# Stores on ScalarE's DMA queue, 25 words later: a fused agent attention and maxout FFN on one core

## The chip, the core and the metric

The kernel runs on one core of one Trainium2 chip. The core has a tensor engine (PE; PEld is its weight load), VectorE (DVE), ScalarE (ACT), GpSimd (POOL) and SyncE (SP), each with its own instruction stream that runs in program order. They meet through semaphores. Data moves between the chip's memory (HBM) and the on-chip SBUF through 16 DMA engines; a DMA is issued as an instruction in one engine's stream, and each issuing engine has a DMA queue of its own. Matmul results land in PSUM.

The metric is the device time of one execution, in microseconds (us): the median of several runs. The profile is of one further execution, and its span runs from the program's first instruction to its last.

## What is computed

```python
def _attn_ref(q, k, v, agents):                      # q, k, v: 4 x 12544 x 128, agents: 4 x 49 x 128
    def sm(a, b):                                    # softmax of scale * a b^T over the last axis
        ...
    agent_v = sm(agents, k) @ v                      # 49 x 128 for each batch
    return sm(q, agents) @ agent_v

def _moe_ref(x, w1, w2, w3, w_out):                  # x: 50176 x 128, w1..w3: 128 x 768, w_out: 768 x 128
    h = np.maximum(np.maximum(x @ w1, x @ w2), x @ w3)
    return h @ w_out
```

The attention's output, 50176 rows of 128, is the input of the FFN. q, k, v are read once and the output is written once, in fp32: four tensors of 25.7 MB each.

## The kernel before

Keys and values of the four batches (b = 0 to 3) are handled in tiles of 7 x 128 rows (`k*b.g`, `v*b.g`), up to four tiles to a load of 1792 KB. Out of them come, for each batch, the 49 agent values and a small matrix G that carries the whole FFN for queries of that batch. Queries are handled in groups s = 0 to 48 of 8 x 128 rows (group 48 holds the last two row blocks of all four batches). One load `ql.z` brings three groups (1536 KB); one store `st` takes three groups away.

A query group goes through these steps, each a word in the program's order:

- `qc` (GpSimd, line 535) casts the loaded rows to bf16; `qt` (PE, line 305) transposes; `qe` (ScalarE, line 541) evacuates.
- `sc` (PE, line 273) gives scores, `ex` (ScalarE, line 554) exponentials, `su` and `re` their sums and reciprocals (VectorE, line 564).
- `u` and `v` (PE) give the hidden values, `a` (ScalarE, line 574) and `x` (VectorE, line 577) the maximum, `p` (PE) the output products.
- `ov.s.0` and `ov.s.1` (VectorE, line 595; for `ov.47.1` ScalarE, line 598) scale them into the output tile OS.
- `st` (line 521, function `store`) issues the DMA from OS to the output. Groups 0 to 44 leave in fifteen stores of three groups (st.2, st.5, ... st.44), groups 45, 46 and 48 in stores of 512 KB, group 47 in two halves.

Loads go to five LD buffers and outputs to five OS buffers: the first `ov` of a new set of three groups waits until the store that last read its buffer has landed. All loads and stores are issued by SyncE, apart from one small load of the agents on ScalarE's queue (line 214).

The order is written out by hand as one text of 1225 words, `ORDER`. Every word is emitted in that order, so the place of a word fixes where its instruction stands in the stream of its engine, and only there: a word's neighbours on other engines do not hold it, semaphores do. A suffix such as `/4` names the buffer. The list `graph` tells each word's engine, its inputs and its tiles; the numbers `cost` and `serve` in it are not used when the order is given.

Of the kernel before, what the change touches and what calls it, by code (L numbers as in the profile page):

```python
# [197 lines left out]
class Emit:  # L198
# [316 lines left out]
    def store(self, s, h=None):  # L515
        def fn():
            n = LONG if s < NQ - 1 - TG else GT
            far, near = self.far("out", s, n), self.near(s, self.t[f"os.{s // TG * TG}"], n)
# [2 lines left out]
            self.nc.sync.dma_start(far, near)
        return fn
# [226 lines left out]
kx1.7/1 kv1.6 a.1/1 su.2 v.1/6 re.2 u.2/0 qc.3/0 kv1.7 x.1/1 a.2/2 v.2/4 p.1/3,1 qc.4/1 x.2/2 qt.3/2 ov.1.0 p.2/7,6 qc.5/2
qe.3/0 ov.1.1 kl1.12/4 ov.2.0 kc1.8/1 sc.3/0 ov.2.1 qt.4/4 ex.3/3 kc1.9/2 kt1.8/3 qe.4/1 vl1.12/1 su.3 u.3/1 ke1.8/1 v.3/2  # L750
kc1.10/0 kt1.9/7 a.3/0 re.3 ks1.8/6 sc.4/4 ke1.9/2 kx1.8/2 kc1.11/1 kt1.10/3 x.3/0 st.2 ex.4/4 ks1.9/0 qt.5/1 ke1.10/0 kx1.9/3
vc1.8/2 su.4 kt1.11/6 qe.5/2 re.4 ks1.10/7 p.3/2,0 ke1.11/1 vc1.9/3 kx1.10/0 kv1.8 ov.3.0/1 sc.5/3 vc1.10/0 kv1.9 ov.3.1
ex.5/5 ks1.11/4 ql.9/0 u.4/1 vc1.11/1 kx1.11/1 kv1.10 a.4/1 su.5 v.4/6 re.5 u.5/7 qc.6/0 kv1.11 x.4/1 a.5/2 v.5/2 p.4/0,4
x.5/2 qc.7/1 qt.6/3 ov.4.0 p.5/1,6 kc1.12/2 qe.6/0 kl2.0/2 ov.4.1 ov.5.0 kc1.13/0 kt1.12/7 sc.6/2 ov.5.1 qt.7/0 vc1.12/2
ke1.12/2 ex.6/6 kt1.13/4 qe.7/1 su.6 vc1.13/3 ks1.12/3 ke1.13/0 u.6/1 v.6/6 re.6 kx1.12/2 sc.7/7 qc.8/2 a.6/0 vl2.0/4 kv1.12
ex.7/7 ks1.13/0 x.6/0 kx1.13/3 qt.8/4 kv1.13 qe.8/2 su.7 p.6/2,3 nr1 u.7/1 v.7/6 re.7 ov.6.0/2 a.7/1 sc.8/0 pu1/4 ov.6.1 pv1/5
ex.8/0 ql.12/1 x.7/1 vs1 qc.9/0 su.8 u.8/7 ub1 v.8/1 re.8 a.8/2 p.7/2,3 tm1 qc.10/1 qt.9/5 ov.7.0 qe.9/0 qc.11/2 ov.7.1 x.8/2
sc.9/6 vb1 kl2.4/3 qt.10/0 rd1 ex.9/1 p.8/7,4 kc2.0/1 qe.10/1 su.9 u.9/2 v.9/3 kc2.1/2 kt2.0/5 a.9/0 sc.10/1 re.9 ke2.0/1
qt.11/0 kc2.2/0 ex.10/2 ov.8.0 kt2.1/2 qe.11/2 ks2.0/6 kc2.3/1 ov.8.1 su.10 kt2.2/5 vl2.4/0 ps1/7 re.10 kx2.0/0 ke2.1/2 u.10/4
pd1 sc.11/0 a.10/1 ke2.2/0 vc2.0/0 ks2.1/1 kt2.3/6 ex.11/3 sl1 ks2.2/2 kx2.1/1 v.10/4 vc2.1/1 kv2.0/5 kx2.2/2 ke2.3/1 su.11  # L760
px1/1 re.11 vc2.2/2 x.9/0 kv2.1 gx1 x.10/1 ks2.3/7 ql.15/2 py1/2 vc2.3/3 kx2.3/3 kv2.2 qc.12/0 gy1 kv2.3 p.9/6,0 qc.13/1
p.10/3,1 ov.9.0/3 qt.12/4 ov.9.1 u.11/7 qc.14/2 qe.12/0 v.11/2 kl2.8/4 ov.10.0 kc2.4/2 ov.10.1 a.11/2 sc.12/6 qt.13/0 x.11/2
ex.12/4 kc2.5/0 kt2.4/3 qe.13/1 su.12 p.11/4,7 ke2.4/2 kc2.6/1 kt2.5/1 re.12 ov.11.0 ks2.4/2 sc.13/0 kc2.7/2 kx2.4/0 ke2.5/0
vl2.8/1 kt2.6/3 ex.13/5 ov.11.1 qt.14/6 vc2.4/0 ks2.5/4 ke2.6/1 su.13 qe.14/2 kt2.7/2 u.12/1 re.13 vc2.5/1 ke2.7/2 kv2.4
kx2.5/1 ks2.6/7 sc.14/3 a.12/0 vc2.6/2 kv2.5 kx2.6/2 ks2.7/0 ex.14/6 v.12/6 vc2.7/3 u.13/2 kx2.7/3 x.12/0 kv2.6 ql.18/3 a.13/1
su.14 v.13/4 re.14 u.14/1 qc.15/0 x.13/1 kv2.7 a.14/2 p.12/7,0 qc.16/1 p.13/6,2 ov.12.0/4 qt.15/3 ov.12.1 qc.17/2 v.14/4
qe.15/0 ov.13.0 kl2.12/0 ov.13.1 sc.15/1 kc2.8/0 x.14/2 qt.16/7 ex.15/7 kc2.9/1 kt2.8/0 qe.16/1 vl2.12/2 su.15 p.14/6,3 ke2.8/0
# [71 lines left out]
```

## Time and profile before

| what | us |
|---|---|
| median of 3 runs | 259.56 (258.92 to 260.03) |
| profiled execution | 258.95 |
| its span | 257.1 |
| PE busy | 187.8 |
| VectorE busy | 166.3 |
| GpSimd busy | 145.6 |
| ScalarE busy | 145.2 |

In the profile an engine with a q behind its name (SPq, ACTq) is its sequencer, which waits and issues. A line of a timeline reads: start, duration, engine, line of the kernel, operation, tile written <- tiles read, shapes, count, and in brackets the idle time before it with what ended that. A line of a group or of the DMA issues ends with the time from issue to landing, which is when the last of the 16 DMA engines has finished its part. In the table of windows the last three columns are the tensor engine's granted clock, the mean busy share of the 16 DMA engines and the bytes that they moved per time.

### The profile page before, as it was taken

How to read it: one execution, taken by the hardware profiler on the slowest of the kernel's cores; microseconds unless marked ns; L12 is line 12 of the kernel's file. 1: busy time of each engine (PE TensorE's matmuls, PEld its weight loads, DVE VectorE, ACT ScalarE, POOL GpSimd, SP SyncE). 2: the span in 40 equal slices, each digit the busy share in tenths (PEclk: the TensorE clock that was granted, in tenths of full speed). 3: DMA queues.
4: the chain of work that ended last, by engine and by line, in shares of the span. 5: the costliest groups of instructions: out<-in, count | busy, mean ns of one | idle time of the engine just before them, and what ended most of it. 6: DMA issues, size and time to landing. Idle time of an engine off the chain costs nothing.

```text
span 257.1 us, 7504 instructions
## 1 busy us (share of the span) xinstructions
PE 187.8 (73%) x3071; PEld 138.0 (54%) x3106; DVE 166.3 (65%) x344; ACT 145.2 (56%) x240; POOL 145.6 (57%) x164
## 2 busy tenths in 40 slices
...
DMA  7999999999999999999999999999999999999992
GB/s 257 435 415 416 427 420 426 420 426 419 420 418 425 423 422 427 424 418 423 418 426 424 419 425 425 426 416 421 424 432 421 421 410 431 423 423 426 410 370 85
DMA packets 11528, 105.01 MB, mean 409 GB/s; under 512 B 1176, under 2 KB 2396, under 8 KB 4444
## 3 DMA queue, kind: packets, MB, share of 16 engines
q1 hardware_dynamic: 11280, 104.34, 97.0%
...
q10 hardware_dynamic: 203, 0.10, 0.1%
q14 instruction: 19, 0.15, 0.1%
...
## 4 chain that ended last, share of the span: by engine, by line
DMA 55%; POOL 12%; PE 12%; DVE 8%; ACT 5%; issue 3%; another core or an unknown queue 1%; SPq 0%; DVEq 0%; ACTq 0%; POOLq 0%
DMA LD<-in_v_dram 25%; DMA LD<-in_k_dram 14%; DMA out_dram<-OS 9%; PE psum L273 9%; POOL VB L300 6%; DMA LD<-in_moe_w_dram 5%; DVE OS L595 3%; POOL KB L300 3%; POOL QB L535 3%; PE psum L305 3%; DMA sums_of<-in_agents_dram 2%; ACT EQ L554 1%; ACT VB L298 1%; ACT QT L541 1%; DVE R L577 1%
## 5 line engine op out<-in xcount | busy, mean ns | idle before, releaser
L300 POOL CAST KB<-LD 128x896 bf16<-128x896 f32 x56 | 51.8, 964 | 36.2 <-DMA LD<-in_k_dram 35.2
L535 POOL CAST QB<-LD 128x1024 bf16<-128x1024 f32 x49 | 49.7, 1048 | 34.7 <-DMA LD<-in_q_dram 26.0
L595 DVE TENSOR_TENSOR OS<-psum,sums_of 128x512 f32<-128x512 f32 x97 | 60.7, 676 | 9.7 <-DMA out_dram<-OS 5.0
L541 ACT ACTIVATE QT<-psum 128x1024 bf16<-128x1024 bf16 x49 | 50.2, 1024 | 21.9 <-PE psum L305 20.2
L311 DVE COPY KT<-psum 128x896 bf16<-128x896 bf16 x56 | 34.5, 620 | 34.0 <-PE psum L305 29.8
L305 PE MATMUL psum<-ident,KB 128*128 128x128 bf16 x392 | 37.8, 249 | 11.3 <-POOL KB L300 10.2
L300 POOL CAST VB<-LD 128x896 bf16<-128x896 f32 x42 | 38.5, 956 | 5.8 <-DMA LD<-in_v_dram 5.4
L554 ACT ACTIVATE EQ<-psum 128x512 bf16<-128x512 f32 x49 | 29.3, 598 | 21.9 <-PE psum L273 15.9
L320 ACT ACTIVATE EK<-psum 128x343 bf16<-128x343 f32 x56 | 25.3, 459 | 25.4 <-PE psum L273 16.6
L305 PEld LDWEIGHTS <-KB 128*128 128x128 bf16 x392 | 29.2, 113 | 17.9 <-POOL KB L300 14.0
L305 PE MATMUL psum<-ident,QB 128*128 128x128 bf16 x392 | 31.9, 228 | 6.5 <-POOL QB L535 5.8
L574 ACT ACTIVATE AS<-psum 128x512 bf16<-128x512 f32 x49 | 29.1, 597 | 12.8 <-PE psum L273 12.3
L577 DVE TENSOR_TENSOR R<-psum,AS 128x512 bf16<-128x512 f32 x49 | 32.4, 676 | 5.8 <-ACT AS L574 2.2
L305 PEld LDWEIGHTS <-QB 128*128 128x128 bf16 x392 | 26.1, 102 | 15.2 <-POOL QB L535 8.4
L273 PEld LDWEIGHTS <-EQ 49*128 49x128 bf16 (+1 forms) x588 | 20.8, 97 | 16.9 <-ACT EQ L554 8.0
L273 PE MATMUL psum<-QT,agT 128*128 128x512 bf16 (+1 forms) x82 | 25.2, 374 | 6.2 <-ACT QT L541 5.7
L273 PE MATMUL psum<-EQ,G 128*128 128x512 bf16 (+1 forms) x91 | 28.0, 367 | 1.3 <-issue 0.6
L273 PEld LDWEIGHTS <-VB 128*128 128x128 bf16 x392 | 16.8, 97 | 17.7 <-ACT VB L298 8.9
L273 PE MATMUL psum<-EK,VB 128*128 128x49 bf16 x392 | 19.6, 187 | 6.4 <-ACT VB L298 5.2
L273 PE MATMUL psum<-agT,KT 128*128 128x49 bf16 x392 | 20.7, 192 | 1.5 <-DVE KT L311 0.9
L273 PE MATMUL psum<-G,EQ 49*128 49x128 bf16 x392 | 20.9, 223 | 1.2 <-DVE OS L595 0.5
L273 PE MATMUL psum<-G,R 64*128 64x128 bf16 x392 | 20.1, 223 | 1.4 <-DVE R L577 1.4
...
## 6 DMA issues: line engine op xcount, KB each, us to landing
LD<-in_q_dram SPq DMA_DIRECT2D x16, 1536.0 KB, 17.7
out_dram<-OS SPq DMA_DIRECT2D x15, 1536.0 KB, 22.1
...
LD<-in_v_dram SPq DMA_DIRECT2D x12, 1792.0 KB, 17.0
LD<-in_k_dram SPq DMA_DIRECT2D x4, 896.0 KB, 16.7
LD<-in_v_dram SPq DMA_DIRECT2D x4, 896.0 KB, 15.0
...
```

The costliest lines, as they stand in the source:

```text
L273: self.nc.tensor.matmul(out, w, x, start=start, stop=True, skip_group_check=True)
L298: self.nc.scalar.activation(out, src, AF.Copy)
L300: self.nc.gpsimd.tensor_copy(out=out, in_=src)
L305: self.nc.tensor.transpose(t[:, j * P:(j + 1) * P], src[:, j, :], self.ident)
L311: return lambda: self.nc.vector.tensor_copy(out=self.t[f"kT{r}"], in_=self.t[f"kT_ps{r}"].bitcast(BF16)[:, :KT * C])
L320: return lambda: self.nc.scalar.activation(self.t[f"e{r}"], self.t[f"s{r}"][:, :KT * A], AF.Exp, scale=SCALE)
L535: return lambda: self.nc.gpsimd.tensor_copy(out=self.t[f"qb.{s}"], in_=self.half("q", s))
L541: return lambda: self.nc.scalar.activation(self.t[f"qT.{s}"].rearrange("p j c -> p (j c)"), self.t[f"qT_ps.{s}"].bitcast(BF16), AF.Copy)
L554: return lambda: self.nc.scalar.activation(self.t[f"e.{s}"], self.t[f"qs.{s}"], AF.Exp, scale=SCALE)
L574: return lambda: self.nc.scalar.activation(self.t[f"a.{s}"], self.t[f"u.{s}"], AF.Relu)
L577: return lambda: self.nc.vector.tensor_tensor(out=self.t[f"r.{s}"], in0=self.t[f"v.{s}"], in1=self.t[f"a.{s}"], op=ALU.max)
L595: self.nc.vector.tensor_tensor(out=out, in0=src, in1=rc.unsqueeze(2).to_broadcast([P, 4, C]), op=ALU.mult)
```

## The change

The fifteen stores of three groups are issued from ScalarE's stream, on its DMA queue, and each of their words stands 25 words later in `ORDER`. The stores of groups 45 to 48 stay with SyncE. No other word changes its place among the rest, and no buffer is given differently.

```diff
         elif alone or s == z + TG - 1:
-            add(f"st.{s}", SP, em.store(s), after=[f"ov.{i}.{o}" for i in ([s] if alone else range(z, z + TG)) for o in range(2)],
+            add(f"st.{s}", SP if alone else ACT, em.store(s), after=[f"ov.{i}.{o}" for i in ([s] if alone else range(z, z + TG)) for o in range(2)],
...
-            self.nc.sync.dma_start(far, near)
+            (self.nc.scalar if s < NQ - 1 - TG else self.nc.sync).dma_start(far, near)
```

In `ORDER` the lines are wrapped anew; what differs in content is the place of the fifteen words. Three of them, with their lines:

```diff
-ov.26.0 p.27/0,1 ov.26.1 qc.30/0 x.28/1 qc.31/1 qt.30/7 x.29/2 p.28/4,2 qe.30/0 kc3.12/0 st.17 sc.30/5 kc3.13/1 kt3.12/3 ex.30/6
...
+sc.31/7 qc.32/2 kv3.12 ql.36/2 ex.31/7 ks3.13/3 u.30/5 kx3.13/3 su.31 a.30/0 st.17 re.31 kv3.13 ov.27.0/4 qt.32/3 ov.27.1
...
-qt.45/2 ex.44/5 ov.48.1 p.42/3,4 qe.45/1 su.44 x.43/2 u.44/7 v.44/1 st.41 re.44 a.44/0 p.43/0,6 sc.45/2 x.44/0 qt.46/5 ex.45/6
...
-qe.47/0 su.46 u.46/0 ov.44.1 v.46/3 a.46/2 re.46 sc.47/6 st.44 x.45/1 ex.47/0 x.46/2 p.45/7,5 su.47 p.46/1,2 ov.45.0/1 u.47/0
...
+st.41 u.46/0 ov.44.1 v.46/3 a.46/2 re.46 sc.47/6 x.45/1 ex.47/0 x.46/2 p.45/7,5 su.47 p.46/1,2 ov.45.0/1 u.47/0 re.47 v.47/4
+ov.45.1 a.47/0 ov.46.0 st.45 ov.46.1 x.47/0 st.46 p.47/3,7 ov.47.1 ov.47.0 st.47.0 st.47.1 c0 c1 good st.44 worst
```

Words such as `qc` or `ov` between the old and the new place stay in the streams of their own engines; on ScalarE a moved store stands behind the `qe`, `ex`, `a` or `kx` that precedes it in the new order. st.44 comes behind `ov.47.1`, ScalarE's last product.

More of the change, by code (lines that the diff above doesn't have):

```diff
@@ L749 @@
[L749 to L767, printed above, removed]
@@ L803 @@
[L803 to L807 removed]
+qc.2/2 py0/6 sc.0/3 kc1.4/0 gy0 qt.1/1 ex.0/0 kc1.5/1 qe.1/1 kt1.4/2 su.0 u.0/7 ke1.4/0 v.0/4 kc1.6/2 a.0/0 kt1.5/0 re.0 ks1.4/6
@@ new lines @@
+sc.1/1 ke1.5/1 kx1.4/2 kc1.7/0 vl1.8/2 kt1.6/2 x.0/0 ex.1/1 ks1.5/3 qt.2/7 ke1.6/2 vc1.4/2 kx1.5/3 su.1 kt1.7/6 qe.2/2 re.1
+ks1.6/0 vc1.5/3 p.0/4,3 ke1.7/0 kx1.6/0 kv1.4 ov.0.0/0 sc.2/2 vc1.6/0 kv1.5 ov.0.1 ex.2/2 ks1.7/1 vc1.7/1 u.1/7 ql.6/3 kx1.7/1
+kv1.6 a.1/1 su.2 v.1/6 re.2 u.2/0 qc.3/0 kv1.7 x.1/1 a.2/2 v.2/4 p.1/3,1 qc.4/1 x.2/2 qt.3/2 ov.1.0 p.2/7,6 qc.5/2 qe.3/0 ov.1.1
+kl1.12/4 ov.2.0 kc1.8/1 sc.3/0 ov.2.1 qt.4/4 ex.3/3 kc1.9/2 kt1.8/3 qe.4/1 vl1.12/1 su.3 u.3/1 ke1.8/1 v.3/2 kc1.10/0 kt1.9/7
@@ new lines @@
+a.3/0 re.3 ks1.8/6 sc.4/4 ke1.9/2 kx1.8/2 kc1.11/1 kt1.10/3 x.3/0 ex.4/4 ks1.9/0 qt.5/1 ke1.10/0 kx1.9/3 vc1.8/2 su.4 kt1.11/6
+qe.5/2 re.4 ks1.10/7 p.3/2,0 ke1.11/1 vc1.9/3 kx1.10/0 kv1.8 ov.3.0/1 sc.5/3 vc1.10/0 kv1.9 ov.3.1 ex.5/5 ks1.11/4 ql.9/0 u.4/1
+st.2 vc1.11/1 kx1.11/1 kv1.10 a.4/1 su.5 v.4/6 re.5 u.5/7 qc.6/0 kv1.11 x.4/1 a.5/2 v.5/2 p.4/0,4 x.5/2 qc.7/1 qt.6/3 ov.4.0
+p.5/1,6 kc1.12/2 qe.6/0 kl2.0/2 ov.4.1 ov.5.0 kc1.13/0 kt1.12/7 sc.6/2 ov.5.1 qt.7/0 vc1.12/2 ke1.12/2 ex.6/6 kt1.13/4 qe.7/1
@@ new lines @@
+su.6 vc1.13/3 ks1.12/3 ke1.13/0 u.6/1 v.6/6 re.6 kx1.12/2 sc.7/7 qc.8/2 a.6/0 vl2.0/4 kv1.12 ex.7/7 ks1.13/0 x.6/0 kx1.13/3
+qt.8/4 kv1.13 qe.8/2 su.7 p.6/2,3 nr1 u.7/1 v.7/6 re.7 ov.6.0/2 a.7/1 sc.8/0 pu1/4 ov.6.1 pv1/5 ex.8/0 ql.12/1 x.7/1 vs1 qc.9/0
+su.8 u.8/7 ub1 v.8/1 re.8 a.8/2 p.7/2,3 tm1 qc.10/1 qt.9/5 ov.7.0 qe.9/0 qc.11/2 ov.7.1 x.8/2 sc.9/6 vb1 kl2.4/3 qt.10/0 rd1
+ex.9/1 p.8/7,4 kc2.0/1 qe.10/1 su.9 u.9/2 v.9/3 kc2.1/2 kt2.0/5 a.9/0 sc.10/1 re.9 ke2.0/1 qt.11/0 kc2.2/0 ex.10/2 ov.8.0
@@ new lines @@
+kt2.1/2 qe.11/2 ks2.0/6 kc2.3/1 ov.8.1 su.10 kt2.2/5 vl2.4/0 ps1/7 re.10 kx2.0/0 ke2.1/2 u.10/4 pd1 sc.11/0 a.10/1 ke2.2/0
+vc2.0/0 ks2.1/1 kt2.3/6 ex.11/3 sl1 ks2.2/2 kx2.1/1 v.10/4 vc2.1/1 kv2.0/5 kx2.2/2 ke2.3/1 su.11 px1/1 re.11 vc2.2/2 x.9/0 kv2.1
+gx1 x.10/1 ks2.3/7 ql.15/2 py1/2 vc2.3/3 kx2.3/3 kv2.2 qc.12/0 gy1 kv2.3 p.9/6,0 qc.13/1 p.10/3,1 ov.9.0/3 qt.12/4 ov.9.1 u.11/7
+qc.14/2 qe.12/0 v.11/2 kl2.8/4 ov.10.0 kc2.4/2 ov.10.1 a.11/2 sc.12/6 qt.13/0 x.11/2 ex.12/4 kc2.5/0 kt2.4/3 qe.13/1 su.12
@@ new lines @@
+p.11/4,7 ke2.4/2 kc2.6/1 kt2.5/1 re.12 ov.11.0 ks2.4/2 sc.13/0 kc2.7/2 kx2.4/0 ke2.5/0 vl2.8/1 kt2.6/3 ex.13/5 ov.11.1 qt.14/6
+vc2.4/0 ks2.5/4 ke2.6/1 su.13 qe.14/2 kt2.7/2 u.12/1 re.13 vc2.5/1 ke2.7/2 kv2.4 kx2.5/1 ks2.6/7 sc.14/3 a.12/0 vc2.6/2 kv2.5
+kx2.6/2 ks2.7/0 ex.14/6 v.12/6 vc2.7/3 u.13/2 kx2.7/3 x.12/0 kv2.6 ql.18/3 a.13/1 su.14 v.13/4 re.14 u.14/1 qc.15/0 x.13/1 kv2.7
+a.14/2 p.12/7,0 qc.16/1 p.13/6,2 ov.12.0/4 qt.15/3 ov.12.1 qc.17/2 v.14/4 qe.15/0 ov.13.0 kl2.12/0 ov.13.1 sc.15/1 kc2.8/0
@@ new lines @@
+x.14/2 qt.16/7 ex.15/7 kc2.9/1 kt2.8/0 qe.16/1 vl2.12/2 su.15 p.14/6,3 ke2.8/0 kc2.10/2 kt2.9/2 re.15 ov.14.0 ks2.8/4 sc.16/7
+kc2.11/0 kx2.8/0 ke2.9/1 kt2.10/0 ex.16/0 ov.14.1 qt.17/1 vc2.8/0 ks2.9/6 ke2.10/2 su.16 qe.17/2 kt2.11/4 u.15/2 re.16 vc2.9/1
+ke2.11/0 ks2.10/3 kv2.8 kx2.9/1 sc.17/0 kx2.10/2 vc2.10/2 a.15/0 kv2.9 ks2.11/7 ex.17/1 v.15/1 ql.21/4 st.5 u.16/4 vc2.11/3
+kx2.11/3 x.15/0 kv2.10 a.16/1 su.17 v.16/6 re.17 u.17/3 qc.18/0 x.16/1 kv2.11 a.17/2 p.15/2,7 p.16/1,4 qc.19/1 ov.15.0/0 qt.18/0
@@ new lines @@
+ov.15.1 v.17/6 kc2.12/1 kl3.0/1 qe.18/0 ov.16.0 kc2.13/2 kt2.12/3 ov.16.1 sc.18/2 ke2.12/1 qt.19/7 vc2.12/0 ex.18/2 x.17/2
+kt2.13/1 qe.19/1 ks2.12/0 vc2.13/1 su.18 ke2.13/2 p.17/4,3 re.18 kx2.12/0 u.18/6 ov.17.0 ks2.13/7 qc.20/2 sc.19/1 a.18/0 vl3.0/0
+ov.17.1 kv2.12 kx2.13/1 v.18/2 ex.19/3 kv2.13 x.18/0 qt.20/0 su.19 nr2 u.19/4 qe.20/2 p.18/6,7 re.19 v.19/3 ov.18.0/1 pu2/2
+a.19/1 pv2/5 sc.20/1 vs2 ov.18.1 ub2 ql.24/2 vb2 ex.20/4 x.19/1 qc.21/0 tm2 su.20 p.19/0,6 qc.22/1 u.20/4 re.20 qt.21/5 ov.19.0
@@ new lines @@
+a.20/2 v.20/7 ov.19.1 qc.23/2 qe.21/0 rd2 kl3.4/3 sc.21/3 qt.22/2 kc3.0/0 ex.21/5 qe.22/1 su.21 u.21/1 x.20/2 kc3.1/1 kt3.0/0
+ps2/4 a.21/0 re.21 sc.22/6 ke3.0/0 kc3.2/2 kt3.1/5 sl2 ex.22/6 ks3.0/7 qt.23/2 kc3.3/0 kx3.0/2 ke3.1/1 vl3.4/4 su.22 kt3.2/3
+qe.23/2 re.22 px2/1 pd2 ke3.2/2 vc3.0/2 ks3.1/0 sc.23/4 gx2 ks3.2/7 kx3.1/3 vc3.1/3 kt3.3/5 kx3.2/0 kv3.0/6 ke3.3/0 ex.23/7
+py2/2 vc3.2/0 kv3.1 gy2 vc3.3/1 su.23 kv3.2 ks3.3/3 re.23 p.20/1,0 kx3.3/1 qc.24/0 v.21/7 ov.20.0 kv3.3 u.22/5 qc.25/1 v.22/2
@@ new lines @@
+v.24/1 u.25/5 ov.22.1 v.25/4 a.25/1 u.26/2 ov.23.0 a.26/2 v.26/3 ov.23.1 qc.27/0 x.24/0 qc.28/1 qt.27/5 x.25/1 p.24/2,7 x.26/2
+qe.27/0 qc.29/2 p.25/0,1 sc.27/4 ql.30/3 qt.28/3 ex.27/3 kc3.8/2 qe.28/1 su.27 u.27/5 re.27 v.27/4 kc3.9/0 a.27/0 kt3.8/3
+sc.28/5 st.11 x.27/0 kc3.10/1 ke3.8/2 ex.28/4 kt3.9/4 kl3.12/4 kc3.11/2 su.28 ke3.9/0 ks3.8/3 kx3.8/2 re.28 ks3.9/4 vc3.8/2
+kt3.10/5 kx3.9/3 qt.29/3 vl3.12/1 ke3.10/1 kt3.11/4 vc3.9/3 qe.29/2 kv3.8 ke3.11/2 ks3.10/5 vc3.10/0 kv3.9 kx3.10/0 sc.29/3
@@ new lines @@
+p.29/7,5 qe.32/2 ov.28.0 v.30/0 u.31/1 ov.28.1 a.31/1 v.31/4 sc.32/3 ov.29.0 ex.32/0 ov.29.1 qc.33/0 su.32 u.32/1 x.30/0 v.32/2
+a.32/2 qc.34/1 re.32 qt.33/7 x.31/1 p.30/5,0 nr3 qe.33/0 qc.35/2 ql.39/4 p.31/3,1 x.32/2 pu3/4 pv3/6 sc.33/7 ub3 st.20 vs3
+ov.30.0/0 qt.34/2 ex.33/1 vb3 ov.30.1 p.32/6,5 qe.34/1 ov.31.0 su.33 u.33/0 a.33/0 sc.34/2 re.33 ov.31.1 ql.48/1 qt.35/3 ex.34/2
+tm3 v.33/7 qe.35/2 su.34 u.34/0 qc.36/0 rd3 v.34/1 a.34/1 sc.35/4 qc.37/1 qt.36/3 ex.35/3 qe.36/0 qc.38/2 re.34 su.35 u.35/0
```

58 lines of the change are left out of this document (18 added, 40 removed).

## The prediction

> **What bounds the kernel now.** I read the page first, for what is full and who ends the chain.
>
> ```profile
> span 257.1 us, 7504 instructions
> ...
> DMA  7999999999999999999999999999999999999992
> GB/s 257 435 415 416 427 420 426 420 426 419 420 418 425 423 422 427 424 418 423 418 426 424 419 425 425 426 416 421 424 432 421 421 410 431 423 423 426 410 370 85
> ...
> q1 hardware_dynamic: 11280, 104.34, 97.0%
> ...
> q10 hardware_dynamic: 203, 0.10, 0.1%
> ...
> DMA 55%; POOL 12%; PE 12%; DVE 8%; ACT 5%; issue 3%; another core or an unknown queue 1%; SPq 0%; DVEq 0%; ACTq 0%; POOLq 0%
> ```
>
> The 16 DMA engines are full in all slices but the first and the last. One queue, q1 (SyncE's), carries 104.34 MB; q10 is ScalarE's, used today for the agents alone. The table of windows shows how the fullness ends.
>
> ```profile
> core 0: us, PE busy (x) PEld busy (x) DVE busy (x) ACT busy (x) POOL busy (x), PEclk, DMA share, GB/s
> 2.00:66.00 64.00, 42.12 (x651) 32.47 (x654) 30.21 (x62) 31.10 (x52) 35.33 (x38) 0.89 1.01 418
> 66.00:187.00 121.00, 97.99 (x1693) 73.56 (x1714) 85.06 (x167) 72.30 (x122) 88.71 (x98) 0.95 1.01 423
> 187.00:227.00 40.00, 35.21 (x550) 24.47 (x557) 33.58 (x72) 30.08 (x48) 17.64 (x20) 0.95 1.01 422
> 227.00:244.00 17.00, 12.31 (x182) 7.46 (x183) 14.05 (x29) 11.09 (x19) 2.85 (x3) 0.95 1.01 422
> 244.00:248.00 4.00, 0.16 (x1) 0.00 (x0) 2.37 (x8) 0.00 (x0) 0.00 (x0) 0.50 1.03 421
> 248.00:251.00 3.00, 0.00 (x0) 0.00 (x0) 0.00 (x0) 0.00 (x0) 0.00 (x0) 0.50 0.70 287
> 251.00:254.50 3.50, 0.00 (x0) 0.00 (x0) 0.00 (x0) 0.00 (x0) 0.00 (x0) 0.50 0.38 132
> ```
>
> Compute is over by 248; the DMA engines are full until then, and some of them work on to 254.5. So the end is bytes over rate, and it moves only if the rate changes or if a DMA engine that finishes last runs out of work before the end. Loads alone (before 66), loads with stores (66 to 227) and stores alone (227 to 244) run at 418 to 423 GB/s, so the mix of kinds is no matter. Next come the rows that tie loads, stores and compute together: from the timelines of GpSimd, VectorE, ScalarE and SyncE, then from the view of the tile OS.
>
> ```profile
> 226.83 3.01 POOL L535 CAST QB<-LD 128x1024 bf16<-128x1024 f32 x3 [4.32 <-DMA LD<-in_q_dram]
> ...
> 179.52 0.69 DVE L595 TENSOR_TENSOR OS<-psum,sums_of 128x512 f32<-128x512 f32 x1 [2.43 <-DMA out_dram<-OS]
> 199.48 0.69 DVE L595 TENSOR_TENSOR OS<-psum,sums_of 128x512 f32<-128x512 f32 x1 [0.29 <-DMA out_dram<-OS]
> 226.61 1.24 DVE L595 TENSOR_TENSOR OS<-psum,sums_of 128x512 f32<-128x512 f32 x2
> 234.00 1.29 DVE L595 TENSOR_TENSOR OS<-psum,sums_of 128x512 f32<-128x512 f32 x2 [0.98 <-DMA out_dram<-OS]
> 235.31 2.43 DVE L595 TENSOR_TENSOR OS<-psum,sums_of 128x512 f32<-128x512 f32 x4
> ...
> 192.31 0.59 ACT L574 ACTIVATE AS<-psum 128x512 bf16<-128x512 f32 x1
> 236.69 1.02 ACT L541 ACTIVATE QT<-psum 128x1024 bf16<-128x1024 bf16 x1
> 242.81 1.14 ACT L598 ACTIVATE OS<-psum,sums_of 128x128 f32<-128x128 f32 x4 [1.95 <-PE psum L273]
> ...
> 175.61 0.42 SPq L521 DMA_DIRECT2D out_dram<-OS  x1
> 203.74 3.27 SPq L521 DMA_DIRECT2D out_dram<-OS  x1
> 237.78 6.70 SPq L521 DMA_DIRECT2D out_dram<-OS  x5
> ```
>
> ```profile
> L521 SPq DMA_DIRECT2D out_dram<-OS x20: 332/396/3270, 68.6 to 244.0; - x20
> ...
>   DMA out_dram<-OS: 5.0, 4
> ...
> DMA to landing us min/median/max: 11.3/19.8/26.6
> ```
>
> The last load is waited for until 226.8, and the casts start with it. A store takes 11.3 to 26.6 us from issue to landing, because it stands behind everything that SyncE has issued. Four times VectorE waits, 5.0 us in all, for an OS buffer whose store has not landed.
>
> **The change part by part.** Bytes, DMAs and arithmetic stay. Fifteen stores of 1536 KB (st.2 to st.44) go to ScalarE's queue, 25 words later. Moved past on SyncE are the loads between the old and the new place, which no longer stand behind them; on ScalarE the activations behind each store now wait for its issue.
>
> *Issue on ScalarE.* SyncE needs 0.396 us in the median (row above), ScalarE needed 0.58 us for its one DMA:
>
> ```profile
> L214 ACTq DMA_DIRECT2D sums_of<-in_agents_dram x1: 576/576/576, 0.7 to 0.7; - x1
> ...
> 200.00:244.00 44.00, 36.30 (x571) 23.75 (x580) 38.94 (x83) 32.85 (x53) 13.91 (x15) 0.98 1.01 421
> ```
>
> Seven of the fifteen (st.23, 26, 29, 32, 35, 38, 41) fall into 200 to 244: 2.8 to 4.0 us. ScalarE idles 44 - 32.85 = 11.1 us there, VectorE 5.1 us, so most is covered; I take half of the lower end, 1.4 us, as delay of compute. Without cover it is all 2.8 to 4.0.
>
> *Waits on ScalarE.* The store waits for the last `ov` of its groups, and behind it ScalarE's evacuations and exponentials would stand. But the place is late: st.41 comes after qe.47 (236.69 + 1.02 = 237.71) and its last product ended at 226.61 + 1.24 = 227.85; st.44 comes after the last activation (242.81 + 1.14 = 243.95) and its products ended by 237.74. Nothing is added: 0.
>
> *When a store lands.* A DMA into an empty queue is shown only by the first load, 896 KB in 5.3 us:
>
> ```profile
> LD<-in_k_dram SPq DMA_DIRECT2D x1, 896.0 KB, 5.3
> ...
> out_dram<-OS SPq DMA_DIRECT2D x1, 1536.0 KB, 23.8
> ...
> out_dram<-OS SPq DMA_DIRECT2D x1, 1536.0 KB, 12.6
> ...
> out_dram<-OS SPq DMA_DIRECT2D x1, 256.0 KB, 11.3
> ```
>
> 896 KB at 422 GB/s is 2.2 us, so 3.1 us are fixed. A store of 1536 KB (1.573 MB) then takes 3.1 + 3.7 = 6.8 us if its ring has the engines to itself, and 3.1 + 7.5 = 10.6 us if loads take every other turn. Take st.17: today issued at 175.61, landed 23.8 later at 199.4, and VectorE's product at 199.48 waits for just that. After, it comes behind a.30 on ScalarE (192.31 + 0.59 = 192.9) and lands at 199.7 to 203.5: 0.3 to 4.1 us late, where a loss of the wait would be a gain of at most its 0.29. I take the middle, 2.2 us: later issue and shorter queue almost cancel. By conservation the loads meet the same sum of work, so the last load stays near 226.8.
>
> *Compute together.* 1.4 + 2.2 = 3.6 us late at 200, against 5.1 us of idle VectorE until 244; I let half of that idle take it up, 2.5, and keep about 1.1 us at the end of compute. The ends are -1.3 (the OS waits at 199.48 and 234.00 gone) and 4.1 + 4.0 = 8.1 (nothing taken up).
>
> *The tail.* st.44 now follows the last activation, where it used to be issued at 237.78 and to land 12.6 us later. With st.47 that leaves 1536 + 512 KB = 2.10 MB, 5.0 us at 422 GB/s, to start at 243.95 at the earliest: 243.95 + 3.1 + 5.0 = 252.0. Today the last store lands at 243.98 + 11.3 = 255.3. So **3.3 us** of delayed compute stay hidden behind the other stores' bytes; 1.1 is less, and the tail adds 0. Past 3.3 us every microsecond shows.
>
> *Two rings at once.* The trace has them together only while the agents load. The view of DMA queues from 2.4 to 4.6 us:
>
> ```profile
> q1 hardware_dynamic: 118, 0.81, 90.2%
> q10 hardware_dynamic: 62, 0.03, 4.9%
> ```
>
> 90.2 + 4.9 = 95.1% leave 4.9% of full, that is 0.049 x 2.2 us x 16 = 1.7 us of engine time for 62 foreign packets, 28 ns each. One store is about 170 packets (1.573 MB over 104.34 MB / 11280), fifteen over 16 engines 159 an engine: at most **+4.5 us**. The other end: if both rings together reached the best slice, 435 in place of 422, over 15 x 7.5 = 112 us, it would be **-3.4 us**. I take 0, by the windows, where a mix of loads and stores ran at the rate of either alone. The Trainium skill (DMA: Bandwidth & Descriptors, Issuing engines are not separate DMA queues) says that issuing from several engines saves only the time of the sequencer; by that rule this term is 0 too, and no run here shows two rings with large packets.
>
> *Sum.* The profiled execution took 258.95 us, 257.1 of it span: 258.95 + 0 (bytes) + 0 (rings) + 0 (tail) = 258.95. The median of the runs is 0.61 above it: **259.6 us**, no change.
>
> **The rivals.**
>
> *A, the tail opens (slower).* OS buffers come back at the late end (4.1 us) and the issues are not covered (2.8): compute ends 6.9 us late, 3.6 past the 3.3 that st.44's new place allows: 259.6 + 3.6 = **263.2**. For it: VectorE is busy 38.94 of 44 us and waits for exactly these buffers. Against: casts that start as a load lands, and two OS waits that might vanish.
>
> *B, ScalarE held at the issue (slower).* The issue at 203.74 took 3.27 us on SyncE, when a store needed up to 26.6 us to land, so some seven DMAs of 3.7 us were outstanding. If ScalarE's issues meet that too, seven cost 22.9 us, 11.1 are idle, and 11.8 - 3.3 = 8.5 show: **268.1**. Against: each ring then holds only its own loads or stores. The Trainium skill (Perfetto Trace Analysis, DMA Instruction — HWDGE (DVE, Sync)) tells of one descriptor generator that two sequencers lock in turn; by that, an issue on SyncE that stalls would hold ScalarE as well; the trace of before, with one DMA from ScalarE, cannot show it.
>
> *C, two rings move more (faster).* -3.4 us: **256.2**. For it only the slice at 435 GB/s; against it the flat 418 to 423. Shorter OS waits alone give nothing, as compute does not set the end.
>
> *D, alternating costs time (slower).* +4.5: **264.1**; the 512-byte packets that price it are the worst case.
>
> That the change does nothing to the traffic is not open: q10 must carry 15 x 1.573 = 23.6 MB.
>
> **How the numbers follow.** Forecast 0.40, A 0.25, B 0.10, C 0.15, D 0.10. Half a percent, 1.3 us, is about what a measurement of this kernel tells from no change: 258.3 to 260.9, which is the forecast's own range. Slower is A + B + D = 0.45, same 0.40, faster 0.15. The range reaches 257.0 (most of C's way) to 264.6 (A and D inside, B outside).
>
> **What would show it.** q10 with 23.6 MB; DMA share still 1.0 from 2 to 248, and the tail as before; the last load waited for until 226 to 229; landings of ScalarE's stores 7 to 11 us; VectorE's OS waits near 5 us. A dip of the share between 244 and 252 is A; ScalarE issues over 1 us each are B; GB/s over 428 or under 418 while stores flow is C or D.

## The result and the profile after

| | before | after |
|---|---|---|
| median of the runs, us | 259.24 (258.73 to 260.03, 4 runs) | 269.43 (268.57 to 269.75, 4 runs) |
| profiled execution, us | 258.95 | 268.57 |
| its span, us | 257.1 | 266.8 |

The change makes the kernel slower: 1.0393 times the time before (95% interval 1.0376 to 1.0411), 10.2 us. The forecast was 259.6, no change, with a range up to 264.6: the prediction was wrong. Ratios and their intervals, here and below, are worked out from runs in the chip's faster state alone, which leaves out one run of the last experiment. The page of after:

```profile
span 266.8 us, 7494 instructions
...
DMA  7999999999999999999999999999999975499992
GB/s 264 439 417 416 429 417 428 420 419 430 413 419 424 436 417 428 418 419 415 432 421 429 416 428 422 431 383 406 417 380 420 425 326 238 179 378 402 410 423 108
...
q1 hardware_dynamic: 9120, 80.74, 72.8%
q10 hardware_dynamic: 2363, 23.69, 21.3%
...
DMA 45%; PE 25%; DVE 8%; POOL 7%; ACT 7%; issue 4%; another core or an unknown queue 0%; POOLq 0%; ACTq 0%; DVEq 0%
PE psum L273 18%; DMA LD<-in_v_dram 14%; DMA out_dram<-OS 13%; DMA LD<-in_k_dram 10%; PE psum L305 7%; DMA LD<-in_q_dram 7%; DVE OS L595 5%; ACT QT L541 4%; POOL KB L300 2%; POOL QB L535 2%; ACT EQ L554 2%; POOL VB L300 2%; DMA sums_of<-in_agents_dram 2%; DVE R L577 1%; DVE sums_of L564 1%
```

q10 carries the stores, 23.69 MB. The row of the DMA engines, full to the last slice before, now has a hole of three slices, 7, 5 and 4 tenths, where 179 GB/s is the lowest. The table of windows of after sizes it:

```profile
core 0: us, PE busy (x) PEld busy (x) DVE busy (x) ACT busy (x) POOL busy (x), PEclk, DMA share, GB/s
...
66.00:187.00 121.00, 98.37 (x1636) 73.23 (x1657) 78.85 (x158) 71.05 (x120) 86.79 (x96) 0.89 1.00 420
187.00:227.00 40.00, 30.43 (x432) 20.24 (x436) 27.70 (x60) 22.34 (x36) 16.18 (x18) 0.87 0.91 370
227.00:244.00 17.00, 15.96 (x261) 10.69 (x263) 15.01 (x31) 14.03 (x21) 6.24 (x6) 1.00 0.73 301
244.00:248.00 4.00, 3.47 (x46) 2.14 (x46) 4.00 (x10) 3.50 (x5) 0.00 (x0) 1.00 1.07 417
```

Until 187 little is lost: 420 GB/s, 423 before. Between 187 and 244 the engines stand empty for 0.09 x 40 + 0.27 x 17 = 8.2 us. Those bytes are moved after 244, and this is most of the 9.7 us by which the span has grown. Why they stand empty, the sequencer of SyncE tells, first before, then after:

```profile
200.07 3.58 SPq L513 DMA_DIRECT2D LD<-in_q_dram  x1
203.74 40.74 SPq L521 DMA_DIRECT2D out_dram<-OS  x11
```

```profile
185.14 17.04 SPq L513 DMA_DIRECT2D LD<-in_q_dram  x5
242.18 13.24 SPq L521 DMA_DIRECT2D out_dram<-OS  x5
```

The last load is issued at nearly the same time (203.7 and 202.2 are the ends of the rows), and SyncE has nothing more to issue until 242.2. In the change that load was issued at 201.9 and landed 14.4 us later, at 216.3; from there to 242 only ScalarE's stores feed the DMA engines, and they come too late. The view of the tile OS and VectorE's timeline of after:

```profile
L521 ACTq DMA_DIRECT2D out_dram<-OS x15: 338/338/385, 74.7 to 253.2; - x15
...
L598 ACT ACTIVATE OS<-psum,sums_of x4: 361/368/378, 253.1 to 253.9; 128x128 f32<-128x128 f32 x4
...
  DMA out_dram<-OS: 14.6, 4
...
DMA to landing us min/median/max: 5.1/9.7/13.8
```

```profile
171.25 1.29 DVE L595 TENSOR_TENSOR OS<-psum,sums_of 128x512 f32<-128x512 f32 x2 [5.68 <-DMA out_dram<-OS]
...
189.66 1.29 DVE L595 TENSOR_TENSOR OS<-psum,sums_of 128x512 f32<-128x512 f32 x2 [4.88 <-DMA out_dram<-OS]
...
203.53 3.68 DVE L595 TENSOR_TENSOR OS<-psum,sums_of 128x512 f32<-128x512 f32 x6 [3.67 <-DMA out_dram<-OS]
...
210.90 1.89 DVE L595 TENSOR_TENSOR OS<-psum,sums_of 128x512 f32<-128x512 f32 x3 [0.40 <-DMA out_dram<-OS]
```

The four products are the first of groups 21, 24, 27 and 30, which wait for st.8, st.11, st.14 and st.17. Before, the same four stood like this (group 24 at 179.52 and group 30 at 199.48 are in the prediction; group 27 waited for no store):

```profile
163.20 1.29 DVE L595 TENSOR_TENSOR OS<-psum,sums_of 128x512 f32<-128x512 f32 x2 [1.32 <-DMA out_dram<-OS]
```

Most of their lateness is there at the first of them, and it grows from turn to turn: 171.25 - 163.20 = 8.05 us at group 21, 189.66 - 179.52 = 10.1 at group 24, 210.90 - 199.48 = 11.4 at group 30. VectorE's waits for OS rise from 5.0 to 14.6 us, and the last activation on OS starts at 253.9, before at 243.6: compute ends **10.3 us late**. The chain of waits of after, from 150 to 215, shows how one wait makes the next:

```profile
158.21 13.01 DMA out_dram<-OS
171.25 0.70 DVE OS L595
...
171.99 3.26 PE psum L273 x20
...
178.91 0.70 ACT QT L541
...
179.68 9.95 DMA out_dram<-OS
189.66 0.70 DVE OS L595
```

st.8 is issued at 158.21, lands 13.0 us later and releases group 21's product. From there the chain runs over matmuls to ScalarE's evacuations, and behind these st.11 is issued, at 179.68, although its own products are long there. It is a loop: late buffer, late product, late evacuation, late store, late buffer.

### The profile page after: what moved, and what is told of

Read it like the earlier page. It is cut to its first block, busy times and chain, and to the rows that moved or that the text cites. A ratio compares the mean times of both kernels' runs of the same rounds, so it can differ in the third digit from the quotient of the medians.

```text
span 266.8 us, 7494 instructions
## 1 busy us (share of the span) xinstructions
PE 193.9 (73%) x3071; PEld 140.8 (53%) x3106; DVE 164.8 (62%) x344; ACT 145.6 (55%) x240; POOL 145.9 (55%) x164
## 3 DMA queue, kind: packets, MB, share of 16 engines
q10 hardware_dynamic: 2363, 23.69, 21.3%
## 4 chain that ended last, share of the span: by engine, by line
DMA 45%; PE 25%; DVE 8%; POOL 7%; ACT 7%; issue 4%; another core or an unknown queue 0%; POOLq 0%; ACTq 0%; DVEq 0%
PE psum L273 18%; DMA LD<-in_v_dram 14%; DMA out_dram<-OS 13%; DMA LD<-in_k_dram 10%; PE psum L305 7%; DMA LD<-in_q_dram 7%; DVE OS L595 5%; ACT QT L541 4%; POOL KB L300 2%; POOL QB L535 2%; ACT EQ L554 2%; POOL VB L300 2%; DMA sums_of<-in_agents_dram 2%; DVE R L577 1%; DVE sums_of L564 1%
## 5 line engine op out<-in xcount | busy, mean ns | idle before, releaser
L595 DVE TENSOR_TENSOR OS<-psum,sums_of 128x512 f32<-128x512 f32 x97 | 60.9, 678 | 19.7 <-DMA out_dram<-OS 14.6
L535 POOL CAST QB<-LD 128x1024 bf16<-128x1024 f32 x49 | 50.5, 1051 | 21.5 <-PE psum L305 17.9
L300 POOL CAST VB<-LD 128x896 bf16<-128x896 f32 x42 | 38.1, 946 | 10.5 <-DMA LD<-in_v_dram 10.5
L305 PE MATMUL psum<-ident,KB 128*128 128x128 bf16 x392 | 35.9, 241 | 9.3 <-POOL KB L300 8.2
L305 PEld LDWEIGHTS <-KB 128*128 128x128 bf16 x392 | 27.8, 109 | 15.0 <-POOL KB L300 10.6
L305 PE MATMUL psum<-ident,QB 128*128 128x128 bf16 x392 | 33.5, 234 | 2.4 <-POOL QB L535 1.7
L273 PEld LDWEIGHTS <-EQ 49*128 49x128 bf16 (+1 forms) x588 | 21.4, 100 | 24.2 <-issue 12.8
L273 PE MATMUL psum<-EQ,G 128*128 128x512 bf16 (+1 forms) x91 | 31.0, 404 | 4.2 <-DVE OS L595 3.3
L305 PEld LDWEIGHTS <-QB 128*128 128x128 bf16 x392 | 27.6, 106 | 11.1 <-issue 2.7
L273 PE MATMUL psum<-QT,agT 128*128 128x512 bf16 (+1 forms) x82 | 26.6, 392 | 6.0 <-ACT QT L541 5.8
L273 PE MATMUL psum<-G,EQ 49*128 49x128 bf16 x392 | 22.2, 236 | 7.7 <-DVE OS L595 7.5
L273 PE MATMUL psum<-EK,VB 128*128 128x49 bf16 x392 | 19.9, 188 | 10.3 <-ACT VB L298 5.2
L273 PE MATMUL psum<-G,R 64*128 64x128 bf16 x392 | 21.5, 233 | 1.4 <-DVE R L577 1.4
## 6 DMA issues: line engine op xcount, KB each, us to landing
LD<-in_q_dram SPq DMA_DIRECT2D x16, 1536.0 KB, 14.4
LD<-in_k_dram SPq DMA_DIRECT2D x12, 1792.0 KB, 15.8
LD<-in_v_dram SPq DMA_DIRECT2D x4, 896.0 KB, 16.3
```

Of the source, the lines that this page charges most:

```text
L273: self.nc.tensor.matmul(out, w, x, start=start, stop=True, skip_group_check=True)
L300: self.nc.gpsimd.tensor_copy(out=out, in_=src)
L305: self.nc.tensor.transpose(t[:, j * P:(j + 1) * P], src[:, j, :], self.ident)
L535: return lambda: self.nc.gpsimd.tensor_copy(out=self.t[f"qb.{s}"], in_=self.half("q", s))
L595: self.nc.vector.tensor_tensor(out=out, in0=src, in1=rc.unsqueeze(2).to_broadcast([P, 4, C]), op=ALU.mult)
```

## The experiments

The theory after this reading: OS buffers come back late, because a store on ScalarE is issued when ScalarE comes to its place, and the place is 25 words later; VectorE's waits then add up, and the DMA engines run dry. The rivals: the second queue as such (transfer or issue) costs the time; or the late places of the last stores do, whatever VectorE waits for.

All medians below stand against the kernel before on the same chip, 258.97 to 258.99 us (that of the change against 259.24). "Profiled" is the time of the one execution that the profile shows; before it was 258.95. It can lie off the median by up to 2.1 us, and the last two columns belong to it: VectorE's waits for OS, and "compute", by how much the last activation on OS starts later than in the profile of before (243.6).

| run | median us | ratio, 95% interval | profiled us | OS waits us | compute, us |
|---|---|---|---|---|---|
| the change | 269.43 | 1.0393 (1.0376 to 1.0411) | 268.57 | 14.6 | +10.3 |
| SyncE's queue, 25 words later | 259.41 | 1.0009 (0.9990 to 1.0029) | 259.00 | 12.8 | +2.0 |
| ScalarE's queue, old places | 259.28 | 1.0009 (0.9997 to 1.0022) | 259.04 | 3.4 | +3.4 |
| the change, st.8, 11, 14 at old places | 264.49 | 1.0210 (1.0187 to 1.0233) | 262.39 | 8.4 | +4.1 |
| ScalarE's queue, earlier places | 260.31 | 1.0052 (1.0034 to 1.0070) | 259.92 | 0 | +4.6 |
| only st.23 to st.44 later | 261.84 | 1.0092 (1.0060 to 1.0125) | 261.84 | 4.0 | +3.5 |
| only st.2 to st.20 later | 265.66 | 1.0253 (1.0204 to 1.0303) | 265.37 | 16.3 | +10.0 |
| the change, six OS buffers | 258.29 | 0.9982 (0.9963 to 1.0002) | 259.49 | 0 | -1.2 |
| its control, five OS buffers | 269.04 | 1.0399 (1.0323 to 1.0475) | 267.48 | 16.6 | +9.1 |
| ScalarE's queue, 12 words later | 259.35 | 1.0013 (0.9997 to 1.0030) | 258.44 | 8.6 | +2.2 |
| before, six OS buffers | 259.61 | 1.0017 (1.0000 to 1.0034) | 259.52 | 0 | -1.9 |
| ScalarE's queue, old places, six OS buffers | 259.27 | 1.0016 (1.0002 to 1.0029) | 259.15 | 0 | +1.3 |
| ScalarE's queue, only st.38, 41, 44 later | 260.19 | 1.0062 (1.0040 to 1.0084) | 258.11 | 3.8 | +1.6 |

### The two parts of the change, each alone

The places of the change with SyncE's queue (`ON_ACT` lists the stores that ScalarE issues; here it is empty):

```diff
-            (self.nc.scalar if s < NQ - 1 - TG else self.nc.sync).dma_start(far, near)
+            (self.nc.scalar if h is None and f"st.{s}" in ON_ACT else self.nc.sync).dma_start(far, near)
```

> All stores stay on SyncE's queue; the fifteen stand 25 words later, as in the change. Theory P (an OS buffer comes back late, VectorE waits, and later stores follow late): each of the first ten stores falls behind one more load of 3.7 to 4.3 us in the one queue, so st.8 lands at about 167 in place of 163.2, VectorE's waits for OS grow from 5 to some 9 to 12 us, and the time is 3 to 6 us over before (262 to 265). Theory Q (the second ring itself costs the time): as before, 258.5 to 260.5. Theory T (the late place of st.44 and st.41 at the end costs it): half of the loss or more, with DMA full until 235.

The queue of the change with the places of before (`ON_ACT` lists the fifteen stores; the edit as against the kernel before):

```diff
-            self.nc.sync.dma_start(far, near)
+            (self.nc.scalar if h is None and f"st.{s}" in ON_ACT else self.nc.sync).dma_start(far, near)
```

> The fifteen stores on ScalarE's queue, at the places that they have before the change. Theory P: ScalarE passes st.8's place some 5 us earlier than the later one, the store lands 13 us after that near 163 to 164, so VectorE's waits for OS stay at 4 to 7 us and the time within 1 us of before (258.5 to 260.5). Theory Q: most of the change's +10 us remains, 266 to 270, and the DMA share or GB/s drops while stores and loads flow together.

Neither part costs anything that can be measured; both together cost 10 us. For the places alone 262 to 265 was expected, which missed. Why the two cost only together, is seen at st.8 and at the product of group 21 that waits for it. The issue of st.8 before, with the places alone, and with the queue alone (sequencers of SyncE, SyncE, ScalarE):

```profile
142.90 0.41 SPq L521 DMA_DIRECT2D out_dram<-OS  x1
```

```profile
148.45 0.42 SPq L521 DMA_DIRECT2D out_dram<-OS  x1
```

```profile
153.38 0.34 ACTq L521 DMA_DIRECT2D out_dram<-OS  x1
```

SyncE runs ahead of the engines that compute: 25 words cost it 5.6 us, while ScalarE reaches the old place 10.5 us later than SyncE does, and the new one, 158.21, 15.3 us later. VectorE's timeline with the places alone, then with the queue alone:

```profile
166.84 1.29 DVE L595 TENSOR_TENSOR OS<-psum,sums_of 128x512 f32<-128x512 f32 x2 [4.14 <-DMA out_dram<-OS]
183.32 1.29 DVE L595 TENSOR_TENSOR OS<-psum,sums_of 128x512 f32<-128x512 f32 x2 [3.79 <-DMA out_dram<-OS]
195.25 3.68 DVE L595 TENSOR_TENSOR OS<-psum,sums_of 128x512 f32<-128x512 f32 x6 [1.72 <-DMA out_dram<-OS]
```

```profile
166.16 1.29 DVE L595 TENSOR_TENSOR OS<-psum,sums_of 128x512 f32<-128x512 f32 x2 [0.76 <-DMA out_dram<-OS]
181.13 1.29 DVE L595 TENSOR_TENSOR OS<-psum,sums_of 128x512 f32<-128x512 f32 x2 [2.63 <-DMA out_dram<-OS]
```

Each alone makes group 21 late by 3.6 and 3.0 us, together by 8.05. With the places alone group 24 is 3.8 us late, so the lateness stays what it was, and OS waits of 12.8 us in all cost nothing. SyncE issued st.11 there at 160.08, before the late product of group 21 (166.84), so that product could not delay it: the loop is not closed. The table of windows with the queue alone:

```profile
66.00:160.00 94.00, 75.66 (x1335) 56.60 (x1332) 65.43 (x134) 57.36 (x97) 70.33 (x78) 0.93 1.01 422
...
187.00:227.00 40.00, 32.27 (x470) 21.60 (x471) 29.53 (x64) 26.09 (x42) 18.96 (x20) 0.91 1.00 418
227.00:244.00 17.00, 15.91 (x261) 10.28 (x260) 15.55 (x32) 13.14 (x21) 3.12 (x3) 1.00 1.00 414
```

Two queues move 422 GB/s where one moved 423, and the engines stay full: the rival of the second queue falls.

### Three stores put back, and all of them earlier

The change, with the three stores behind which VectorE waited longest at their places of before; the line of st.8 in the new order:

```diff
+sc.23/4 gx2 ks3.2/7 kx3.1/3 vc3.1/3 kt3.3/5 kx3.2/0 kv3.0/6 ke3.3/0 ex.23/7 py2/2 vc3.2/0 kv3.1 gy2 st.8 vc3.3/1 su.23 kv3.2
```

> The change, but st.8, st.11 and st.14 at their old places (still on ScalarE's queue). Theory P: these three held OS buffers that VectorE waited for; waits for OS fall from 14.6 to about 5 us, and at least 6 of the 10 us come back: 259.5 to 263. Theory Q: no difference from the change, 268 to 270. Theory T: no difference either, the last stores are as late as in the change.

All fifteen on ScalarE's queue, 25 words earlier than before, or as far as their products allow:

```diff
+kt3.1/5 sl2 ex.22/6 ks3.0/7 qt.23/2 kc3.3/0 kx3.0/2 st.8 ke3.1/1 vl3.4/4 su.22 kt3.2/3 qe.23/2 re.22 px2/1 pd2 ke3.2/2 vc3.0/2
```

> The fifteen stores on ScalarE's queue, 25 words earlier than before the change (st.2, st.32 to st.44 as early as their last product allows). Theory P: stores land earlier, VectorE's waits for OS fall to under 2 us, the loads are pushed back by up to one store; the end stays set by bytes over rate: 257.5 to 260. Theory Q: as slow as with the old place on ScalarE, 265 or more.

Three stores of fifteen carry about half of the loss, 4.9 of 10.2 us, but not all, and less than the 6 that were expected: the wait moves on to the next late store, st.17, as VectorE's timeline with the three put back shows.

```profile
205.27 1.89 DVE L595 TENSOR_TENSOR OS<-psum,sums_of 128x512 f32<-128x512 f32 x3 [4.20 <-DMA out_dram<-OS]
```

With early places no wait for OS is left, yet nothing is gained: 260.31 where 257.5 to 260 was expected. The loss of 1.3 us goes with a compute that ends 4.6 us late; what made that late was not followed up.

### Early half, late half

```diff
+sc.23/4 gx2 ks3.2/7 kx3.1/3 vc3.1/3 kt3.3/5 kx3.2/0 kv3.0/6 ke3.3/0 ex.23/7 py2/2 vc3.2/0 kv3.1 gy2 st.8 vc3.3/1 su.23 kv3.2
...
+su.46 st.41 u.46/0 ov.44.1 v.46/3 a.46/2 re.46 sc.47/6 x.45/1 ex.47/0 x.46/2 p.45/7,5 su.47 p.46/1,2 ov.45.0/1 u.47/0 re.47 v.47/4
```

All fifteen are on ScalarE's queue, st.23 to st.44 alone 25 words later (the lines of st.8 and st.41 in the new order).

> The change, but st.2 to st.20 at their old places; only st.23 to st.44 stand 25 words later, all fifteen on ScalarE's queue. Theory P (late return of OS buffers to VectorE, up to the product of group 30, is the loss): waits for OS below 5 us, compute ends no more than 4 us after that of before, time 259 to 262. Theory S (stores leave ScalarE too late, so the DMA engines run out of stores once the loads are done, and the bytes are left for the end): DMA share well below 1.0 between 200 and 235, time 264 or more.

The same with st.2 to st.20 alone 25 words later:

```diff
+qc.26/2 x.22/1 ql.27/1 p.21/0,5 st.8 a.23/2 sc.24/7 kc3.4/1 qt.25/4 x.23/2 ex.24/0 p.22/2,3 kc3.5/2 qe.25/1 su.24 kt3.4/1 re.24
...
+x.42/1 a.43/2 sc.44/5 ov.48.0/4 qt.45/2 ex.44/5 ov.48.1 p.42/3,4 qe.45/1 su.44 x.43/2 u.44/7 v.44/1 st.41 re.44 a.44/0 p.43/0,6
```

> The other half: st.2 to st.20 stand 25 words later, st.23 to st.44 at their old places, all on ScalarE's queue. Theory P: the OS waits at groups 21, 24 and 27 remain, 10 us or more in all, compute ends 7 to 10 us late, time 265 to 268. Theory S: the late stores leave in time, DMA stays full after 200 and the time is 259 to 262.

The early half costs 6.7 us, the late half 2.85; together 9.5 of the 10.2. So the loop of the early stores is the larger part, and there is a second loss at the end. The windows with the late half alone show it as a share of the DMA engines:

```profile
187.00:227.00 40.00, 31.77 (x462) 21.77 (x469) 29.50 (x64) 26.14 (x42) 18.96 (x20) 0.87 0.94 394
227.00:244.00 17.00, 15.50 (x255) 10.31 (x256) 15.55 (x33) 13.14 (x21) 3.12 (x3) 1.00 0.97 392
```

0.06 x 40 + 0.03 x 17 = 2.9 us of empty engines, which is the loss, though compute is late by 3.5 us only, as with the queue alone, where nothing was lost.

### A sixth buffer

The change with six OS buffers. To make room for the sixth, four other sets are smaller; the buffers are given out anew along the same order.

```diff
-SLOTS = {"M": 8, "LD": 5, "QB": 3, "KB": 3, "VB": 4, "KT": 3, "QT": 3, "EQ": 8, "EK": 4, "AS": 3, "R": 3, "OS": 5}
+SLOTS = {"M": 8, "LD": 5, "QB": 3, "KB": 3, "VB": 3, "KT": 3, "QT": 2, "EQ": 6, "EK": 3, "AS": 3, "R": 3, "OS": 6}
```

> The change with six OS buffers in place of five; to make room QT has 2, EQ 6, VB 3 and EK 3 buffers. Beside the next run, which has the same smaller buffers and five OS. Theory P: the waits for OS fall from some 14 to under 3 us, and 6 us or more come back against the next run. Theory S: the waits fall too, but the DMA engines still run out between 220 and 235, and less than 3 us come back.

The control has the smaller sets and `"OS": 5`.

> The change with five OS buffers and the smaller QT, EQ, VB and EK of the run with six. If the smaller buffers cost nothing it is as the change, 268.5 to 270; they may cost up to 3 us more.

Queue, places and smaller sets are the same in both; the sixth buffer alone takes back 269.04 - 258.29 = 10.7 us. The view of OS and the windows with six buffers, then the windows of the control:

```profile
L598 ACT ACTIVATE OS<-psum,sums_of x4: 359/368/376, 241.6 to 242.4; 128x128 f32<-128x128 f32 x4
...
DMA to landing us min/median/max: 9.4/12.5/19.3
```

```profile
187.00:227.00 40.00, 34.37 (x548) 23.74 (x553) 33.02 (x72) 30.18 (x48) 17.28 (x19) 0.97 1.00 419
227.00:244.00 17.00, 11.69 (x181) 7.11 (x183) 15.38 (x30) 10.97 (x19) 3.01 (x3) 0.99 1.00 414
```

```profile
187.00:227.00 40.00, 32.06 (x450) 21.06 (x457) 28.92 (x63) 23.60 (x38) 15.53 (x17) 0.84 0.89 372
227.00:244.00 17.00, 15.86 (x269) 10.95 (x267) 15.05 (x31) 13.84 (x22) 5.20 (x5) 1.00 0.75 306
```

With six buffers no product waits for a store, the engines stay full, and the late places cost nothing, those of the late half included. This is the run that shows the cause: not the queue and not the places in themselves, but the time that a buffer is away, measured against how many buffers there are.

### How far the places may go, and whether six buffers are worth having

All fifteen on ScalarE's queue, 12 words later than before:

```diff
+re.23 p.20/1,0 kx3.3/1 qc.24/0 v.21/7 ov.20.0 kv3.3 u.22/5 st.8 qc.25/1 v.22/2 ov.20.1 a.22/1 qt.24/4 x.21/0 u.23/3 qe.24/0 v.23/1
```

> The change with 12 words in place of 25, five OS buffers. Theory P: ScalarE passes st.8's and st.11's places some 2 us earlier than in the change, so waits for OS are between the 3.4 us of the old place and the 14.6 us of the change, and the time between theirs: 261 to 265. If it is not the place but some single word of the order, it is near one of the two ends.

Nothing is lost, where 261 to 265 was expected. VectorE's timeline with 12 words, then with 25 words for the early half:

```profile
168.63 1.29 DVE L595 TENSOR_TENSOR OS<-psum,sums_of 128x512 f32<-128x512 f32 x2 [3.58 <-DMA out_dram<-OS]
184.41 1.29 DVE L595 TENSOR_TENSOR OS<-psum,sums_of 128x512 f32<-128x512 f32 x2 [2.05 <-DMA out_dram<-OS]
```

```profile
168.37 1.29 DVE L595 TENSOR_TENSOR OS<-psum,sums_of 128x512 f32<-128x512 f32 x2 [5.76 <-DMA out_dram<-OS]
187.74 1.29 DVE L595 TENSOR_TENSOR OS<-psum,sums_of 128x512 f32<-128x512 f32 x2 [6.41 <-DMA out_dram<-OS]
```

Both start equally late at group 21. Before, groups 21 and 24 were 16.3 us apart (163.20, 179.52). With 12 words this turn of the loop takes 15.8 us, and the lateness shrinks; with 25 it takes 19.4, in the change 18.4, and the lateness grows. The turn is made of two parts, the time from the late product to the issue of st.11, and the time from there to its landing. The chains of waits, 12 words first, then the early half, show the second:

```profile
173.53 10.86 DMA out_dram<-OS
```

```profile
176.25 11.47 DMA out_dram<-OS
```

The landings are nearly equal, 10.9 and 11.5 us. The issue comes 173.53 - 168.63 = 4.9 us after the late product with 12 words, 176.25 - 168.37 = 7.9 with 25, and 179.68 - 171.25 = 8.4 in the change: the place makes the turn long. The granted clock between 168 and 188 was 0.83 with 12 words, 0.84 in the early half and 0.83 in the change, so it is not the clock that parts them. Where the turn is no longer than the pace of the groups, the waits cost nothing.

The sixth buffer with the kernel before, and with the queue alone (edits as above):

> Before the change (SyncE's queue, old places), with six OS buffers and smaller QT, EQ, VB and EK. The end is set by bytes over rate, so no OS wait is worth anything there: 258 to 260, waits for OS under 1 us. If the waits set the end, 2 us or more come off.

> ScalarE's queue, old places, six OS buffers. As the run with six OS and later places (258.3) or up to 1 us off it: 257.5 to 259.5; a lead over before of more than 0.5% would say that two rings move more.

No wait for OS is left in either, and the kernel before ends compute 1.9 us earlier; neither gains anything, since the DMA engines were full as it was. No version tried is shown to be faster than before: the best, the change with six buffers, has an interval that reaches to 1.0002.

Last, the queue alone, with only st.38, st.41 and st.44 moved 25 words later:

> All fifteen on ScalarE's queue, old places, but st.38, st.41 and st.44 25 words later. The late half alone cost 2.9 us at a compute end 3.3 us late. If that was st.44 behind the last product, it is here too: 261 to 262.5. If it was the DMA engines running low between 200 and 227, with st.23 to st.35 late, then it is not here: 258.8 to 260, as with all at the old place.

The three cost 260.19 - 258.97 = 1.2 us, between the two results that were expected, with runs from 258.11 to 262.38. By the intervals they cost 1.0 to 2.2 us and the whole late half 1.6 to 3.2; these overlap, so how the loss is shared between the last three and st.23 to st.35 stays open. The profiled execution, 258.11, is the fastest run of this kernel and does not show the loss.

## Why the prediction was wrong

- **What bounds the kernel: right.** The end is bytes over rate unless the DMA engines run dry. In the change they run dry for 8.2 us, and in four runs where they lost under 1 us of work (the places alone, the queue alone, 12 words, six buffers) the time stayed within 0.3%. It is not the whole account: the early places lost 0.03 x 17 = 0.5 us between 187 and 244 and took 1.3 us longer.
- **Issue on ScalarE: small, as said.** 0.338 us in the median and 0.385 at most, below the 0.396 to 0.58 that the prediction used. Rival B needed issues of 3.27 us and is refuted. The Trainium skill (Perfetto Trace Analysis, DMA Instruction — HWDGE (DVE, Sync)) tells of a generator that two sequencers lock in turn; no issue of ScalarE here shows such a hold. No run puts it to the test either: with stores on ScalarE, SyncE's own issues took 1.4 us at most (1.366, with the queue alone), not 3.
- **Two rings: 0, right.** With the queue alone both moved 418 to 424 GB/s while loads and stores flowed, and the ratio was 1.0009; rivals C and D fall. The Trainium skill (DMA: Bandwidth & Descriptors, Issuing engines are not separate DMA queues) says that issuing from several engines saves only the sequencer's time; the 1.0009 agrees. The Trainium skill (Perfetto Trace Analysis, DMA Optimizations) also says that loads on one engine and stores on another may make sense, above all with loops; none of the runs with that split is shown to gain.
- **When a store lands: too early.** Beside loads st.8 took 13.0 us, above the 10.6 of equal shares. The bounds of 6.8 and 10.6 did not hold it.
- **Compute together: this step failed.** It took +1.1 us, with an upper bound of 8.1; it was +10.3. It reckoned the lateness of one store, st.17, and let VectorE's idle time take up half. But the lateness starts three stores earlier, at st.8, and is passed on: each late product delays ScalarE's next place for a store. VectorE's idle time took up none of it: the waits rose by 9.6 us, and compute ended 10.3 later. What should have been reckoned, from rows of before, is the turn of the loop against the pace of the groups. That stores on ScalarE are issued later than on SyncE at the same place was not reckoned for st.8, where it makes 10.5 us of the 15.3. For st.17 it was, from the rows of before, as an issue at 192.9; st.17 left at 199.37, after group 24's product had come 10.1 us late.
- **The last load stays near 226.8: wrong.** Conservation holds for the sum of loads and stores. Late stores left the engines to the loads, which were through early, and nothing was left to fill 202 to 242.
- **The tail: too small, and its 3.3 us rest on a working that the runs do not bear out.** The rule was 3.3 us of late compute hidden and all past it shown. Against the profiled execution of before the change lost 268.57 - 258.95 = 9.6 us, and the rule gives 10.3 - 3.3 = 7.0. The 2.6 that are left are near what the late places of the last stores cost by themselves, a term that the prediction put at 0: the late half alone lost 2.9, where the rule gives 0.2, and the three put back lost 3.4, where it gives 0.8. With the last stores not late nothing is left: the early places lost 1.0 and the early half 6.4, where the rule gives 1.3 and 6.7. But the 3.3 was worked out with st.44 behind the last activation, and in these two runs it does not stand there; that the same number fits them is luck as far as the runs show.
- **Rival A named the mechanism** (buffers late, tail open, a dip in the DMA share), but at 3.6 us and with the dip at 244 to 252. The dip came at 210 to 244: loads end early, so it opens before the tail.

The granted clock between 187 and 227 also fell, from 0.95 to 0.87. The queue alone ran there at 0.91 without loss, and VectorE's waits end with a landing, not with a matmul. Where the turns of 12 and 25 words part, the clock was the same (0.83 and 0.84). So the clock is not needed for the loss, but no run held it fixed.
